# A new order of issue for the attention stage, with longer DMA times, later factor products and a third tile for values

## The chip, the core and the metric

The kernel runs on one core of one Trainium2 chip. The metric is the device time of one execution in microseconds (us), from the chip itself. The core has five engines that each take their instructions in order: TensorE (PE, matrix products and transposes), VectorE (DVE), ScalarE (ACT), GpSimd (POOL) and SyncE (SP), whose only work here is to issue DMAs. An instruction that waits holds back what stands behind it on its engine.

## What is computed

Attention over pooled queries, then a mixture of four experts, then a feed-forward layer with ELU; all in float32:

```python
q_pool = q.reshape(B, H, S // 2, 2, D).mean(axis=3)          # B 2, H 8, S 1152, D 64
scores = np.matmul(q_pool, k.transpose(0, 1, 3, 2)) / np.sqrt(D)
scores = scores - np.max(scores, axis=-1, keepdims=True)
attn = np.exp(scores)
attn = attn / (np.sum(attn, axis=-1, keepdims=True) + 1e-09)
x = np.matmul(attn, v)                                       # then (B*S/2, H*D) = (1152, 512)
for e in range(4):                                           # experts: w1 (512, 1024), w2 (1024, 512)
    out += p[:, e:e + 1] * (np.maximum(x @ w1[e], 0.0) @ w2[e])
h = out @ w_in                                               # (512, 2048)
y = np.where(h > 0.0, h, np.exp(np.minimum(h, 0.0)) - 1.0) @ w_out
```

## The kernel before

The 16 heads are treated as 8 pairs. A pair's 2 x 576 pooled queries are nine blocks of 128; block 4 belongs to both heads. For each block the scores against 1152 keys are made in two parts (z = 0 of 512 columns, z = 1 of 2 x 320), so there are 72 x 2 parts. Every step of the attention has a letter, and each letter a function:

- S `scores` (PE), R `max_all` (DVE, the row maximum of a part), E `exp` (ACT, reads the part from PSUM, 144 of them in all), T `transposes` (PE, three 128 x 128 at a time), D and G `evac` (copies of the transposed blocks to `pt`, on ACT or DVE), V `values` (PE, `pt` with the head's v, in two halves h = 0, 1, line 621), O `output` (ACT or DVE, copies a half of the values from PSUM to the tile `xo`).
- Since the two parts of a row have maxima and sums of their own, each head has a small chain that makes the factors: I (DVE, line 569), U (POOL), J (ACT, exponential of the differences, line 578), K (POOL), M (DVE, reciprocal), N (POOL). The factors must be laid along the free dimension, which is done through DRAM: "3" `factors_out` (SP, `dr<-st`, line 643) and, once that has landed, "4" `factors_in` (SP, two DMAs `fb<-dr`, line 649).
- X `x_scaled` (POOL; DVE for the last two heads) multiplies `xo` by `fb` and adds the two halves, H `x_high` (ACT, `xs<-xo`) rounds the result to the fast format, L `x_low` (POOL) makes the remainder, m `x_out` (SP, four DMAs to `XH` and `XL`) puts both where the experts read them.
- For the next pairs: q and k (SP) load, A, B, C make the high and low part of the queries and r (SP, `Q<-q`, line 488, four DMAs) lays them out; F, W and s (SP, `K<-kh`, `K<-k`, line 505, four DMAs) do so for the keys; v (SP) loads values. w, y, g, f load and split the first weights of the experts.

POOL and DVE copies and products of two tensors come through two helpers, so many of these steps bear line 332 (copy) or 335 (two tensors); the tiles tell them apart.

The order in which all these steps are issued is made by `order_of`, a list scheduler that runs when the kernel is built. `STAGES` gives for each letter the engines that may do it, with the time that the scheduler reckons, and a rank; `LAG` and `LATE` tell how long after its end a step's result is reckoned to be there (SP: the DMA's landing); `MORE` adds to the rank of single steps. The numbers are only the scheduler's: they change no instruction, only its place and, where two engines may do it, its engine. After the attention stand the matrix products of experts and feed-forward (line 798), with `hh` (ACT) and `hl` (DVE) splitting each result; two PSUM tiles take turns there.

Two `xo` tiles took turns by head, so O of a head waited for L of the head two before it.

Of the kernel before, what the change touches and what calls it, by code (L numbers as in the profile page):

```python
# [10 lines left out]
F32 = mybir.dt.float32  # L11
# [7 lines left out]
P = 128  # L19
# [15 lines left out]
    "M": (dict(DVE=200), 1.2),  # L35
    "N": (dict(POOL=400), 1.2),
    "3": (dict(SP=500), 2),
    "4": (dict(SP=950), 2),
    "X": (dict(POOL=2180), 6),
    "T": (dict(PE=327), 2),  # L40
    "D": (dict(ACT=480, DVE=557), -3),
    "G": (dict(ACT=480, DVE=557), -4),
    "V": (dict(PE=2140), 6),
    "O": (dict(ACT=400, DVE=460), 0),
    "H": (dict(ACT=400), 8),
    "L": (dict(POOL=740), 3),
    "a": (dict(POOL=800, DVE=470), 5),
    "b": (dict(ACT=440), 1),
    "c": (dict(DVE=470), 4),
# [3 lines left out]
    "k": (dict(SP=450), -9),  # L53
    "A": (dict(POOL=1430), -4),
    "B": (dict(ACT=690), -4),
    "C": (dict(DVE=1100), -3),
    "r": (dict(SP=1850), -3),
    "F": (dict(ACT=690, DVE=470), -4),
    "W": (dict(POOL=1430), -3),
    "s": (dict(SP=1850), -3),  # L60
    "m": (dict(SP=1850), 8),
    "l": (dict(SP=730), 20),
    "v": (dict(SP=450), -4),
    "w": (dict(SP=730), 20),
    "y": (dict(SP=600), 20),
    "g": (dict(ACT=575), 20),
    "f": (dict(POOL=1365), 20),
# [1 line left out]
}  # L69
WARM = 11  # L70

LAG = {"PE": 190, "ACT": 210, "DVE": 220, "POOL": 210, "SP": 8500}
LATE = {"3": 11000, "4": 8500, "r": 6000, "s": 6000}

MIXED = {"D": dict(ACT=320, DVE=330), "G": dict(ACT=320, DVE=330)}
SECOND = {"S": dict(PE=585), "R": dict(DVE=822), "E": dict(ACT=920), "V": dict(PE=2620)}
# [10 lines left out]
VBANK = "S0", "S0"  # L87

MORE = {
# [16 lines left out]
}  # L106


# [19 lines left out]
def attention_ops(NH, KC):  # L128
# [3 lines left out]
    def op(rank, before, x, *k, after=0):  # L132
        rank += STAGES[x][1] + sum(MORE.get(y, 0) for y in names_of(x, *k))
        ops[(x, *k)] = [b for b in before if b], rank, after
# [27 lines left out]
    for b in range(NB):  # L162
        p, m = divmod(b, MB)

        hs = [2 * p] * (m < 5) + [2 * p + 1] * (m > 3)
        if p:
            need = early = [("r", p), ("s", p)]
        else:
            need = [(x, i, z) for x in "ce" for i in hs for z in range(2)]
            if b < 2:  # L170
                need.remove(("c", 0, 1))
            early = [x for x in need if b > 3 or x != ("e", 0, 1)]
        for z in (0, 1):
            op(b + 0.3 * z, need if z else early, "S", b, z)
            op(b + 0.3 * z, [("S", b, z)], "R", b, z)
            op(b + 0.3 * z, [("R", b, z), *[("T", b - NP, u) for u in U if b >= NP]], "E", b, z)
        for u in U:
            op(b, [("E", b, z) for z in (0, 1) if (z == 0 and 3 * u < CUT) or (z and 3 * u + 3 > CUT)] + [("V", i - 2, 1) for i in hs if i > 1], "T", b, u)
            op(b, [("T", b, u)], "D", b, u)
            if m == 4:  # L180
                op(b, [("T", b, u)], "G", b, u)
        if m in (4, 8):
            i = hs[0]
            for h in (0, 1):
                cs = range(CUT, KC) if h else range(CUT)
                ds = [("D", x, u) for x in blocks_of(i) for u in sorted({c // 3 for c in cs})]
                if i % 2:
                    ds = [("G", *x[1:]) if x[1] == blocks_of(i)[0] else x for x in ds]
                op(b + 0.5 * h, ds + [("V", i, 0) if h else ("v", i)], "V", i, h)
                op(b + 0.5 * h, [("V", i, h)] + [("L", i - 2)] * (i > 1), "O", i, h)  # L190
            op(b, [("E", x, z) for x in range(b - 4 + i % 2, b + 1) for z in (0, 1)], "I", i)
            op(b, [("I", i)], "U", i)
            op(b, [("U", i)], "J", i)
            op(b, [("J", i)], "K", i)
            op(b, [("K", i)], "M", i)
            op(b, [("M", i)], "N", i)
            op(b, [("N", i), i > 1 and ("4", i - 2)], "3", i)
            op(b, [("3", i), i % 2 and ("3", i - 1), i > 1 and ("X", i - 2)], "4", i)
            op(b, [("O", i, 0), ("O", i, 1), ("4", i)], "X", i)
            op(b, [("X", i), i > 1 and ("m", i - 2)], "H", i)  # L200
            op(b, [("H", i)], "L", i)
            op(b, [("L", i)], "m", i)
# [84 lines left out]
def attention_then_moe_then_elu_ffn(  # L287
# [43 lines left out]
    def copy(e, out, a):  # L331
        (nc.scalar.copy if e == "ACT" else engines[e].tensor_copy)(out, a)  # L332

    def tt(e, out, a, b, op):
        engines[e].tensor_tensor(out=out, in0=a, in1=b, op=op)  # L335
# [37 lines left out]
    with ExitStack() as actx:  # L373
# [117 lines left out]
                    )  # L491

        def pair_k_high(e, p, y):
            if y == 0:
                raws["h", p] = raw_p.tile([P, 2, KQ], F32R, tag="k", name="kh")
            copy(e, raws["h", p][:, y], raws["k", p][:, y])

# [130 lines left out]

        xo = [x_p.tile([P, 2, HQ], F32, name="xo%d" % j) for j in range(2)]
        xs = [x_p.tile([P, 2, HQ], F32R, name="xs%d" % j) for j in range(2)]
        fb = [x_p.tile([P, 2 * HQ], F32, name="fb%d" % j) for j in range(2)]

        def output(e, i, h):
            copy(e, xo[i % 2][:, h], tb.pop((i, h))[:, :HQ])

        def factors_out(e, i):
            p, y = divmod(i, 2)
# [12 lines left out]
                )  # L652

        def x_scaled(e, i):
            x = xo[i % 2]
            tt(e, x, x, fb[i % 2].rearrange("p (q z) -> p z q", z=2), ALU.mult)
            tt(e, x[:, 0], x[:, 0], x[:, 1], ALU.add)

        def x_high(e, i):
            copy(e, xs[i % 2][:, 0], xo[i % 2][:, 0])  # L660

        def x_low(e, i):
            x = xs[i % 2]
            tt(e, x[:, 1], xo[i % 2][:, 0], f(x)[:, 0], ALU.subtract)

        def x_out(e, i):
            b, h = heads[i]
# [285 lines left out]
```

## Time and profile before

| | |
|---|---|
| median of 3 runs | 871.22 us (870.48 to 871.96) |
| profiled execution, its own time | 871.93 us |
| its span, first to last instruction | 870.2 us |
| attention, by PE | 0 to 265.2 us |
| experts and feed-forward | 265.2 to 870.2 us |
| PE busy | 850.6 us (98%) |
| DVE, ACT, POOL busy | 473.0, 343.5, 387.8 us |
| mean granted TensorE clock | 0.992 |

A row of the timeline gives the start and length in us, the engine, the line, what is written and read, and in brackets how long the engine had been idle and what ended that. Lines "x3" are several instructions in one row. Everything of the change lies in the attention.

### The profile page before, as it was taken

The numbers are of one execution on the slowest core, as the hardware profiler recorded it, in microseconds if no ns is written. First come the engines' busy times: TensorE is split into PE (matmuls) and PEld (weight loads), VectorE is DVE, ScalarE is ACT, GpSimd is POOL, SyncE is SP. The second block draws the span as 40 slices with busy tenths as digits, with TensorE's granted clock in tenths as the row PEclk, the third lists the DMA queues.
The fourth block names the chain that finished last, engine by engine and source line by source line (L and its number), as shares of the span: only waits on it lengthen the run. The fifth ranks groups of instructions, "written<-read, shape, count | busy, mean of one in ns | idle before, by whom it ended". The sixth has DMA issues, their size and how long they took to land.

```text
span 870.2 us, 13813 instructions
## 1 busy us (share of the span) xinstructions
PE 850.6 (98%) x5374; PEld 793.0 (91%) x5374; DVE 473.0 (54%) x700; ACT 343.5 (39%) x731; POOL 387.8 (45%) x384
## 2 busy tenths in 40 slices
PE   8989999989999999999999999999999999999998
PEld 7767677767768999999999999999999999999998
DVE  8767577666653465564565465465556522333232
ACT  6767686667762312212211221221232243223121
POOL 4343552344323515465554546455454464425321
PEclk9999999999999999999999999999999999999999
DMA  7979858868315424133424315232422311000011
GB/s 255 206 169 198 206 136 190 176 118 206 73 29 168 177 79 160 37 121 122 149 85 132 111 39 173 95 121 98 144 85 86 122 49 49 1 1 1 1 42 69
DMA packets 51457, 97.35 MB, mean 112 GB/s; under 512 B 14912, under 2 KB 29248, under 8 KB 48448
## 3 DMA queue, kind: packets, MB, share of 16 engines
q1 hardware_dynamic: 51392, 96.47, 40.3%
q8 instruction: 42, 0.69, 0.4%
q14 instruction: 23, 0.19, 0.1%
HBM read 64.37 MB, written 10.84 MB: 86 GB/s over the span
## 4 chain that ended last, share of the span: by engine, by line
PE 79%; DMA 9%; POOL 3%; DVE 2%; issue 2%; ACT 2%; SPq 2%; POOLq 0%; DVEq 0%; ACTq 0%
PE p L798 64%; PE t L598 5%; PE s L536 5%; PE s L621 5%; DMA q<-in_q 2%; DMA fb<-dr 2%; DMA Q<-q 2%; POOL xo L335 1%; DMA k<-in_k 1%; POOL acc L853 1%; DMA K<-k 1%; SPq L505 1%; DMA k<-in 1%; ACT e L553 1%; SPq L488 1%
## 5 line engine op out<-in xcount | busy, mean ns | idle before, releaser
L798 PE MATMUL p<-XH,h 128*128 128x384 f32 (+1 forms) x608 | 198.2, 326 | 0.9 <-ACT xo L332 0.5
L798 PE MATMUL p<-XH,l 128*128 128x384 f32 (+1 forms) x608 | 198.0, 326 | 0.0
L798 PE MATMUL p<-XL,h 128*128 128x384 f32 (+1 forms) x608 | 198.0, 326 | 0.0
L798 PE MATMUL p<-hh,l 128*128 128x384 f32 (+1 forms) x608 | 197.9, 326 | 0.0
L798 PE MATMUL p<-hl,h 128*128 128x384 f32 (+1 forms) x608 | 197.9, 326 | 0.0
L798 PE MATMUL p<-hh,h 128*128 128x384 f32 (+1 forms) x608 | 197.9, 326 | 0.0
L335 POOL TENSOR_TENSOR l<-w,h 128x512 fp32r<-128x512 f32 x96 | 125.6, 1326 | 74.2 <-ACT h L332 74.2
L819 ACT ACTIVATE hh<-p 128x768 fp32r<-128x768 f32 (+1 forms) x50 | 39.4, 789 | 280.3 <-PE p L798 280.3
L820 DVE SCALAR_TENSOR_TENSOR hl<-p,hh 128x768 fp32r<-128x768 f32 (+1 forms) x50 | 46.3, 925 | 151.3 <-ACT hh L819 151.3
L798 PEld LDWEIGHTS p<-XH,h 128*128 128x128 f32 x608 | 114.1, 188 | 1.7 <-ACT xo L332 1.0
L798 PEld LDWEIGHTS p<-hh,h 128*128 128x128 f32 x608 | 114.1, 188 | 0.0
L798 PEld LDWEIGHTS p<-hl,h 128*128 128x128 f32 x608 | 114.1, 188 | 0.0
L798 PEld LDWEIGHTS p<-hh,l 128*128 128x128 f32 x608 | 114.1, 188 | 0.0
L798 PEld LDWEIGHTS p<-XL,h 128*128 128x128 f32 x608 | 114.1, 188 | 0.0
L798 PEld LDWEIGHTS p<-XH,l 128*128 128x128 f32 x608 | 114.1, 188 | 0.0
L547 DVE TENSOR_REDUCE st<-s 128x1 f32<-128x512 f32 (+1 forms) x144 | 105.1, 751 | 15.8 <-PE s L536 12.7
L536 PE MATMUL s<-K,Q 128*128 128x320 f32 (+1 forms) x480 | 112.8, 364 | 0.6 <-ACT e L553 0.6
L598 PEld LDWEIGHTS t<-ident,e 128*128 128x128 f32 x648 | 77.4, 144 | 36.4 <-ACT e L553 12.0
L598 PE MATMUL t<-ident,e 128*128 128x128 f32 x648 | 97.3, 282 | 13.3 <-ACT pt L332 7.3
L553 ACT ACTIVATE e<-s,st 128x512 f32<-128x512 f32 (+1 forms) x144 | 107.1, 751 | 1.7 <-DVE st L547 1.6
L772 POOL TENSOR_TENSOR nt<-nt,ne 128x512 f32<-128x512 f32 x32 | 41.8, 1307 | 121.8 <-issue 63.8
L832 POOL TENSOR_TENSOR hl<-e,hh 128x768 fp32r<-128x768 f32 (+1 forms) x26 | 44.8, 1725 | 110.2 <-ACT hh L831 110.1
(68 smaller groups left out, 965.7 us busy)
## 6 DMA issues: line engine op xcount, KB each, us to landing
w<-in_wb SPq DMA_DIRECT2D x8, 1024.0 KB, 6.5
d<-in_va SPq DMA_DIRECT2D x16, 512.0 KB, 4.7
w<-nt SPq DMA_DIRECT2D x32, 256.0 KB, 3.3
d<-in_vb SPq DMA_DIRECT2D x16, 512.0 KB, 4.4
w<-w SPq DMA_DIRECT2D x8, 1024.0 KB, 6.6
Q<-q SPq DMA_DIRECT2D x28, 288.0 KB, 6.2
w<-in_wa SPq DMA_DIRECT2D x7, 1024.0 KB, 6.3
v<-in_v SPq DMA_DIRECT2D x16, 288.0 KB, 6.1
```

The lines of the kernel that those rows point to most:

```text
L335: engines[e].tensor_tensor(out=out, in0=a, in1=b, op=op)
L488: nc.sync.dma_start(out=f(qs[p % 2])[D * r : D * r + D, :, :, half(z)], in_=raws["q", p][D * z : D * z + D],)
L536: nc.tensor.matmul(out=t[:, j], lhsT=q[:, o : o + P], rhs=ks[p % 2][:, y, c : c + PARTS[z][1]], start=k == x == 0, stop=2 * k + x == last,)
L547: nc.vector.tensor_reduce(out=nm[b, z], in_=s_t[b, z], axis=AX.XY, op=ALU.max, negate=True)
L553: nc.scalar.activation(et[b % NP][:, part(z)].rearrange("p (j k) -> p j k", j=PARTS[z][0]), s_t.pop((b, z)), AF.Exp, bias=nm.pop((b, z)), ...
L598: nc.tensor.transpose(t[:, c * P : c * P + P], et[b % NP][:, (3 * u + c) * P : (3 * u + c + 1) * P], ident)
L621: nc.tensor.matmul(out=tb[i, h][64 * z : 64 * z + 64, :HQ], lhsT=raws[i, "v"][:, c, :], rhs=pt[i % 2][:, c, half(z)], start=c == cs[0], st ...
L772: nc.gpsimd.tensor_tensor(out=t, in0=t, in1=e, op=ALU.add)
L798: nc.tensor.matmul(out=ps, lhsT=w[:, c, m * P : m * P + P], rhs=x[:, c], start=c == 0 and w is hi and x is xh, stop=c == 3 and w is lo,)
L819: nc.scalar.activation(oh, s, AF.Relu)
L820: nc.vector.scalar_tensor_tensor(out=ol, in0=s, scalar=0.0, in1=f(oh), op0=ALU.max, op1=ALU.subtract)
L832: nc.gpsimd.tensor_tensor(out=ol, in0=e, in1=f(oh), op=ALU.subtract)
```

## The change

Numbers of the scheduler are changed, and with them the order. The core of the diff:

```diff
-    "4": (dict(SP=950), 2),
-    "X": (dict(POOL=2180), 6),
+    "4": (dict(SP=1700), 2),
+    "X": (dict(POOL=2300), 6),
...
-    "r": (dict(SP=1850), -3),
+    "r": (dict(SP=2400), -3),
...
-LAG = {"PE": 190, "ACT": 210, "DVE": 220, "POOL": 210, "SP": 8500}
-LATE = {"3": 11000, "4": 8500, "r": 6000, "s": 6000}
+LAG = {"PE": 190, "ACT": 210, "DVE": 220, "POOL": 210, "SP": 9500}
+LATE = {"3": 12000, "4": 11500, "r": 8000, "s": 8000, "X": 1200, "U": 900, "K": 700}
...
-                op(b + 0.5 * h, [("V", i, h)] + [("L", i - 2)] * (i > 1), "O", i, h)
+                op(b + 0.5 * h, [("V", i, h)] + [("L", i - 3)] * (i > 2), "O", i, h)
...
-            if y == 0:
+            if ("h", p) not in raws:
...
-        xo = [x_p.tile([P, 2, HQ], F32, name="xo%d" % j) for j in range(2)]
+        xo = [x_p.tile([P, 2, HQ], F32, name="xo%d" % j) for j in range(3)]
...
-            copy(e, xo[i % 2][:, h], tb.pop((i, h))[:, :HQ])
+            copy(e, xo[i % 3][:, h], tb.pop((i, h))[:, :HQ])
```

H, L, C, s, m and w have longer reckoned times too (C a shorter one), the other uses of `xo` count by three, and the table `MORE` is another one throughout. No step is added or left out. All line numbers after 87 grow by one.

Three places show what it makes of the order. On ACT, where head 8 is rounded (`xs<-xo`). Before, that row stands ahead of the exponential of head 10's differences (`st12_119`, step J) and behind 102 of the 144 exponentials of scores (`e..<-s..`):

```order
L553 ACTIVATE e1_98,st11_118<-s10_108,st10_117 128x640
L332 CAST xs0_124<-xo0_122 128x288
L578 ACTIVATE st12_119<-st12_119 128x10
L553 ACTIVATE e0_97,st11_118<-s11_109,st10_117 128x640
L332 COPY pt0_102<-t1_105 128x3x128
L332 COPY pt1_103<-t0_104 128x3x64
L553 ACTIVATE e1_98,st11_118<-s00_106,st10_117 128x512
```

In the changed kernel, at the same head (its `xo` is now the third tile, `xo2`), with two casts of weights (`h<-w`) ahead:

```order
L554 ACTIVATE e3_100,st11_118<-s10_108,st10_117 128x640
L333 CAST h_1759<-w_162 128x512 x2
L333 COPY pt1_103<-t0_104 128x3x128
L579 ACTIVATE st12_119<-st12_119 128x10
L333 CAST xs0_125<-xo2_124 128x288
L333 COPY pt1_103<-t1_105 128x3x128
L554 ACTIVATE e2_99,st01_115<-s00_106,st00_114 128x512
```

The cast has moved behind the exponential of head 10's differences, and stands behind 108 exponentials of scores. Counted in the same way, it moved from 31 to 36 for head 0, from 48 to 57 for head 2 and from 84 to 93 for head 6.

On SP, the first two heads' factors (`dr<-st` out, `fb<-dr` in) among the loads of pairs 2 and 3. Before:

```order
L405 DMA k<-in_k 128x1152
L488 DMA Q_110<-q 64x4x288 x4
L643 DMA dr<-st_116 128x5x2
L405 DMA q<-in_q 128x1152
L409 DMA v<-in_v 128x576
L643 DMA dr<-st_116 128x4x2
L405 DMA q<-in_q 128x1152
L677 DMA p<-in_p 128x36
L505 DMA K_112<-kh 64x2x576 x2
L505 DMA K_112<-k 64x2x576 x2
L649 DMA fb_126<-dr 64x576 x2
L649 DMA fb_127<-dr 64x576 x2
```

In the changed kernel:

```order
L644 DMA dr<-st_116 128x5x2
L410 DMA v<-in_v 128x576
L406 DMA k<-in_k 128x1152
L489 DMA Q_110<-q 64x4x288 x4
L406 DMA q<-in_q 128x1152
L678 DMA p<-in_p 128x36
L644 DMA dr<-st_116 128x4x2
L650 DMA fb_127<-dr 64x576 x2
L406 DMA q<-in_q 128x1152
L506 DMA K_112<-kh 64x2x576 x2
L506 DMA K_112<-k 64x2x576 x2
```

The first head's factors are now read back ahead of the second load of queries and of the copies of keys, no longer behind them; the store of the same factors goes out ahead of pair 2's load of keys.

On DVE, where the attention ends and the experts begin: the products with factors of heads 14 and 15, then the splits `hl` of the experts' first results. Before:

```order
L588 RECIPROCAL st_118<-st_118 128x4
L332 COPY pt_103<-t_104 128x3x128
L335 TENSOR_TENSOR xo_122<-xo_122,fb_126 128x576
L335 TENSOR_TENSOR xo_122<-xo_122 128x288
L335 TENSOR_TENSOR xo_123<-xo_123,fb_127 128x576
L335 TENSOR_TENSOR xo_123<-xo_123 128x288
L820 SCALAR_TENSOR_TENSOR hl<-p_2749,hh 128x2x288
L820 SCALAR_TENSOR_TENSOR hl<-p_2776,hh 128x2x288
```

In the changed kernel:

```order
L589 RECIPROCAL st_118<-st_118 128x4
L336 TENSOR_TENSOR xo_124<-xo_124,fb_127 128x576
L336 TENSOR_TENSOR xo_124<-xo_124 128x288
L821 SCALAR_TENSOR_TENSOR hl<-p_2750,hh 128x2x288
L336 TENSOR_TENSOR xo_122<-xo_122,fb_128 128x576
L336 TENSOR_TENSOR xo_122<-xo_122 128x288
L821 SCALAR_TENSOR_TENSOR hl<-p_2777,hh 128x2x288
```

Head 15's product now stands between the first and the second split. And on SP, in the same place, before:

```order
L643 DMA dr_2553<-st12_119 128x4x2
L649 DMA fb0_126<-dr_2553 64x576 x2
L649 DMA fb1_127<-dr_2553 64x576 x2
L672 DMA XH_67<-xs0_124 64x288
L672 DMA XL_68<-xs0_124 64x288
```

and in the changed kernel:

```order
L644 DMA dr_2598<-st12_119 128x4x2
L650 DMA fb0_127<-dr_2598 64x576 x2
L673 DMA XH_67<-xs1_126 64x288
L673 DMA XL_68<-xs1_126 64x288
L673 DMA XH_67<-xs1_126 64x288
L673 DMA XL_68<-xs1_126 64x288
L650 DMA fb1_128<-dr_2598 64x576 x2
```

Head 15's factors (`fb1`) are read back behind the four DMAs that put out head 13 (`xs1`), whose cast on ACT now stands behind the last copy of values, that of head 15 (`xo`, step O).

## Rows read from the trace of the kernel before

**Rows 1.** The page, first part: busy time, share of the span, instructions by engine

```profile
PE 850.6 (98%) x5374; PEld 793.0 (91%) x5374; DVE 473.0 (54%) x700; ACT 343.5 (39%) x731; POOL 387.8 (45%) x384
```

**Rows 2.** Timeline of PE, 54 to 188 us: all rows with idle time before

```profile
54.79 0.73 PE L536 MATMUL s<-K,Q 128*128 128x512 f32 x2 [0.63 <-ACT e L553]
61.95 0.90 PE L598 MATMUL t<-ident,e 128*128 128x128 f32 x3 [3.16 <-ACT e L553]
...
89.18 0.55 PE L598 MATMUL t<-ident,e 128*128 128x128 f32 x3 [0.49 <-ACT pt L332]
91.00 0.55 PE L598 MATMUL t<-ident,e 128*128 128x128 f32 x3 [1.28 <-ACT pt L332]
...
153.19 1.35 PE L598 MATMUL t<-ident,e 128*128 128x128 f32 x6 [1.97 <-ACT pt L332]
...
187.28 1.31 PE L598 MATMUL t<-ident,e 128*128 128x128 f32 x6 [2.98 <-ACT pt L332]
```

**Rows 3.** Stretches of 40 us: busy by engine, granted clock, DMA share, GB/s

```profile
60.00:100.00 40.00, 36.29 (x241) 28.54 (x243) 25.18 (x48) 28.85 (x76) 19.73 (x32) 0.91 0.83 178
...
140.00:180.00 40.00, 38.03 (x264) 30.65 (x262) 29.19 (x50) 28.98 (x78) 12.99 (x23) 0.96 0.81 164
180.00:220.00 40.00, 37.02 (x255) 28.14 (x254) 24.75 (x50) 28.47 (x76) 20.46 (x36) 0.96 0.70 163
```

**Rows 4.** Timeline of PE: first value product of heads 1, 5, 7, 11

```profile
37.59 2.16 PE L621 MATMUL s<-pt,v 128*64 128x288 f32 x16
...
106.17 2.16 PE L621 MATMUL s<-pt,v 128*64 128x288 f32 x16
...
135.63 2.16 PE L621 MATMUL s<-pt,v 128*64 128x288 f32 x16
...
202.81 2.16 PE L621 MATMUL s<-pt,v 128*64 128x288 f32 x16
```

**Rows 5.** Timeline, 173 to 187 us: head 8's factors, product, cast, next exponential

```profile
173.42 1.11 SPq L649 DMA_DIRECT2D fb<-dr  x2
...
183.11 1.43 POOL L335 TENSOR_TENSOR xo<-xo,fb 128x576 f32<-128x576 f32 x1 [18.22 <-DMA fb<-dr]
...
185.44 0.43 ACT L332 CAST xs<-xo 128x288 fp32r<-128x288 f32 x1 [4.21 <-POOL xo L335]
...
185.99 0.78 ACT L553 ACTIVATE e<-s,st 128x640 f32<-128x640 f32 x1
```

**Rows 6.** Timeline, other engines, at the three earlier stalls

```profile
51.98 1.42 POOL L335 TENSOR_TENSOR q<-q 128x576 f32<-128x576 f32 x1 [5.15 <-DMA p<-in_p]
...
60.68 0.43 ACT L332 CAST xs<-xo 128x288 fp32r<-128x288 f32 x1 [3.79 <-POOL xo L335]
...
87.33 0.43 ACT L332 CAST xs<-xo 128x288 fp32r<-128x288 f32 x1 [1.72 <-POOL xo L335]
...
89.11 0.86 DVE L332 CAST kh<-k 128x576 fp32r<-128x576 f32 x2 [3.58 <-DMA k<-in_k]
...
151.35 0.43 ACT L332 CAST xs<-xo 128x288 fp32r<-128x288 f32 x1 [3.21 <-POOL xo L335]
```

**Rows 7.** Timeline, 263 to 272 us: from the attention to the experts

```profile
263.19 1.09 SPq L649 DMA_DIRECT2D fb<-dr  x2
...
264.75 0.40 ACT L332 COPY xo<-s 128x288 f32<-128x288 f32 x1 [1.97 <-PE s L621]
...
265.20 0.40 PE L798 MATMUL p<-XH,h 128*128 128x288 f32 x1 [0.50 <-ACT xo L332]
...
267.64 0.76 DVE L335 TENSOR_TENSOR xo<-xo,fb 128x576 f32<-128x576 f32 x1
...
270.27 0.59 SPq L672 DMA_DIRECT2D XL<-xs  x1
...
270.44 0.76 DVE L820 SCALAR_TENSOR_TENSOR hl<-p,hh 128x576 fp32r<-128x576 f32 x1 [1.05 <-ACT hh L819]
...
271.83 0.65 ACT L819 ACTIVATE hh<-p 128x576 fp32r<-128x576 f32 x1 [1.42 <-PE p L798]
```

More of the change, by code (lines that the diff above doesn't have):

```diff
@@ L44 @@
     "O": (dict(ACT=400, DVE=460), 0),
-    "H": (dict(ACT=400), 8),
-    "L": (dict(POOL=740), 3),
+    "H": (dict(ACT=440), 8),
+    "L": (dict(POOL=810), 3),
     "a": (dict(POOL=800, DVE=470), 5),
@@ L55 @@
     "B": (dict(ACT=690), -4),
-    "C": (dict(DVE=1100), -3),
-    "r": (dict(SP=1850), -3),
+    "C": (dict(DVE=800), -3),
+    "r": (dict(SP=2400), -3),
     "F": (dict(ACT=690, DVE=470), -4),
     "W": (dict(POOL=1430), -3),
-    "s": (dict(SP=1850), -3),
-    "m": (dict(SP=1850), 8),
+    "s": (dict(SP=2800), -3),
+    "m": (dict(SP=2300), 8),
     "l": (dict(SP=730), 20),
     "v": (dict(SP=450), -4),
-    "w": (dict(SP=730), 20),
+    "w": (dict(SP=1700), 20),
     "y": (dict(SP=600), 20),
@@ L654, in x_scaled @@
         def x_scaled(e, i):
-            x = xo[i % 2]
+            x = xo[i % 3]
             tt(e, x, x, fb[i % 2].rearrange("p (q z) -> p z q", z=2), ALU.mult)
@@ L659, in x_high @@
         def x_high(e, i):
-            copy(e, xs[i % 2][:, 0], xo[i % 2][:, 0])
+            copy(e, xs[i % 2][:, 0], xo[i % 3][:, 0])
         def x_low(e, i):
             x = xs[i % 2]
-            tt(e, x[:, 1], xo[i % 2][:, 0], f(x)[:, 0], ALU.subtract)
+            tt(e, x[:, 1], xo[i % 3][:, 0], f(x)[:, 0], ALU.subtract)
         def x_out(e, i):
```

33 rows, old and new, of the table MORE are left out of this document.

## The prediction

> **What bounds the kernel now.** I read the page's busy times first, then the rows in which PE had been idle, then the granted clock by stretches, and last the other engines around each gap. PE is busy for 98% of the span [rows 1], so only two things can be won: its idle time, and time in which it ran at the lower clock. Between 54 and 188 us six rows show all its idle time there: 0.63 + 3.16 + 0.49 + 1.28 + 1.97 + 2.98 = 10.5 us, each ended by an exponential or a copy on ACT [rows 2]. The clock falls in the same places: 0.91, 0.96 and 0.96 in the three stretches of 40 us that hold the four stalls [rows 3], and it is whole in the others. A clock of 1.2 instead of 2.4 GHz for 9%, 4% and 4% of 40 us is 40 x 0.17 = 6.8 us. So the stalls cost about 17.3 us. A second view agrees: the same value product of heads 5 and 7, a pair apart with no stall between, stands 29.46 us apart; from head 1 to head 11, five pairs, it takes 165.22 us [rows 4], which is 165.22 - 5 x 29.46 = 17.9 us more than five undisturbed pairs. I count 17.3 and leave the odd 0.6.
>
> What stands behind the gaps is the same thing four times. At 187 us: head 8's factors are asked for at 173.42, POOL waits for them until 183.11, ACT has meanwhile reached the cast of the product and stands 4.21 us, and the exponential that PE needs stands right behind that cast [rows 5]. At 60.68, 87.33 and 151.35 the cast of heads 0, 2 and 6 waits 3.79, 1.72 and 3.21 us for POOL; at 89 us DVE also waits 3.58 us for pair 4's keys [rows 6]. Waits of 4.21 and 3.21 on ACT became 2.98 and 1.97 on PE [rows 2, 5, 6]: about 1.24 us of each is covered by what PE has in hand.
>
> **The change part by part.** *The cast later.* No instruction is added. Eighteen exponentials go by in 29.46 us, so one is 1.64 us [rows 4]. By the order, the cast of heads 0, 2, 6 and 8 moves back by 5, 9, 9 and 6 exponentials: 8.2, 14.7, 14.7 and 9.8 us. Against it goes the later issue of the factors' DMA on SP, which I count by the score parts that precede, on PE, the last thing that SP must wait for there: 20 becomes 22, 37 becomes 39, 73 becomes 76, 92 becomes 94, so 3.3, 3.3, 4.9 and 3.3 us. With the wait to be covered that leaves 8.2 - 3.3 - 3.79 = 1.1 us, 14.7 - 3.3 - 1.72 = 9.7, 14.7 - 4.9 - 3.21 = 6.6 and 9.8 - 3.3 - 4.21 = 2.3 us to spare. Head 0's is more than that, since its DMA no longer stands behind a load that waits for a free tile and behind the eight copies of queries and keys; all four waits go. What is behind the cast on ACT is then no longer held; behind the cast itself wait x_low on POOL and four DMAs on SP, and nothing that PE needs within a pair.
>
> *Keys of pair 4.* Their cast on DVE moves behind 58 row maxima instead of 50, 13.1 us; the load moves behind a load of values that waits for a value product ending at about 87 us, where it was issued at about 80: 7 us. 13.1 - 7 - 3.58 leaves 2.5 us. This wait goes too.
>
> *The clock.* It fell in the stretches with the four large gaps of PE and in no others [rows 2, 3]. With the gaps gone I take the 6.8 us as gained.
>
> *The third tile and the later products.* Output of a head waits for x_low three heads back instead of two. With casts later by 5 to 9 exponentials that is what keeps the tile from becoming the new wait; by itself I cost it at nothing, since in all pairs without a late DMA PE shows no idle row. Products on POOL stand further behind in its queue, ahead of the sums and reciprocals of the next heads at a few places (head 2 and 3's two products in a row, 4.5 us). The reciprocals on DVE that wait for POOL there stand beside value products of 2.16 us and more [rows 4], which cover them. If that cover were gone, each would cost PE its length less 1.24 us.
>
> *First 24 us.* The order there changes too. DVE sets the pace, and up to the thirteenth row maximum the same DVE work stands in it but for one cast given to ACT, some 0.4 us. I count nothing, with 1.5 us either way.
>
> *The end of the attention.* Here the change adds a wait. Head 15's factors are asked for behind the four DMAs of head 13, whose cast now stands behind the last output copy on ACT. That copy ends at 265.15 [rows 7]. In the time of the kernel before: cast 0.43 and four issues of about 0.6 us with x_low between, so the factors are asked for at about 268.4, where it was 263.19. From that to the product it was 267.64 - 263.19 = 4.45 us, so the product starts at 272.85, takes 1.2 to 1.75 us, and the second `hl`, which now stands behind it on DVE and lasts 0.76, ends at about 275.4. PE needs that PSUM tile for its fourth group: two groups end before 271.83 [rows 7], some 3.2 us each, so at 274.7. That gives 0.7 to 0.8 us of new idle time. Its bounds: none, if the factors come 0.8 us sooner; and 6.0 us, if they take the 9.7 us that they took at 173.42 [rows 5]. I take 0.8, because the 4.45 us are from the same place, where few other DMAs run. The first `hl` stays ahead of the product, and the experts' own loads, behind head 15's DMAs on SP, come about 4 us later, at the second of their uses.
> The Trainium skill's page "DMA: Bandwidth & Descriptors" (section "Anatomy of one DMA") gives one DMA, there fitted for GpSimd's, a fixed 2.0 us and its bytes at 436 GB/s. By it an estimate for these 147 KB is 2.3 us; the end would then cost nothing and the time would be 0.8 us less. Both rows here differ from it.
>
> **Sum.** The profiled execution took 871.93 us, of which 870.2 are its span; that is 0.7 above the median of 871.22. 871.93 - 10.5 - 6.8 + 0.8 = 855.4, and from the median 871.22 - 16.5 = 854.7 us.
>
> **The rivals.**
> 1. *The loads of the first pairs.* Pair 4's queries are now asked for behind head 0's factors, and POOL adds them between the differences and the sum of head 2. In the kernel before, POOL stood 5.15 us for them, until 51.98 [rows 6] (the row names a small load issued right behind them). If they land some 2 us later than that, the reciprocal of head 2 on DVE waits, and the first stall stays: 0.63 + 3.16 us and half of the first stretch's clock loss, 1.8, so 5.6 us: 860.3. For it: the DMA share there is the highest. Against: nothing but two factor DMAs was put ahead of it.
> 2. *The spare is too small.* Heads 0 and 8 have 1.1 and 2.3 us. If factors land later than they did by more than that plus the cover of 1.24, each stalls again, by about 1 us and a fall of the clock of 1.7 (6.8 / 4): 5.4 us together, 860.1.
> 3. *The end.* Factors of head 15 that take 9.7 us: 5.2 us more and one fall of the clock, 861.7.
> 4. *POOL becomes the bound of each pair's end, and it is slower.* POOL's run there (two splits of keys, a product, the sums of two heads) holds a reciprocal on DVE, and row maxima stand behind it. At a stall like that at 187 us, 2.98 + 1.7 = 4.7 us at each of seven pair ends is 32.8 us, so 887.5. It decides from 2.6 us for each, idle and clock together, because 7 x 2.6 = 18.2 is the gain and the 0.2%; so from a wait of about 2.1 us on DVE. Against it: POOL is busy 45% [rows 1], and in the pair from 106 to 136 us its waits left no idle row on PE.
>
> **How the numbers follow.** The forecast has 0.66, with a range of its own from 851.5 (no new wait at the end, 1.5 us from the start, the odd 0.6) to 858. Rival 1 has 0.12, rival 2 0.10, rival 3 0.08, rival 4 0.04. The range from 851.5 to 862.5 takes in the forecast and the first three. A measurement of this kernel can tell about 0.2% from no change, 1.7 us. All cases but the fourth are faster by more than that: 0.96. Rival 4 gives 0.03 to slower and 0.01 to no change.
>
> **What would show it.** PE's rows with idle time between 40 and 250 us should be gone or under 0.6 us, the granted clock should be 1.00 in every stretch, and the value products of all pairs should stand 29.5 us apart. Casts of products on ACT should have no idle time ahead that ends with POOL, and POOL's products none that ends with a factor DMA. The matrix products of the experts should begin some 17 us earlier, with one gap of about 0.8 us some 9.5 us later, ended by `hl`. Wrong would be: a fall of the clock anywhere after 40 us, reciprocals on DVE that wait over 2 us for POOL with PE idle behind them, or a long wait of DVE for the last factors.

## The result, and the profile after

The changed kernel takes 856.45 us (median of 4 runs, 855.12 to 857.05), the kernel before 870.85 us beside it: a ratio of 0.9842 (95% interval 0.9819 to 0.9865), 14.4 us less. The forecast was 854.7 us, 16.5 less. Of the profiled executions one took 871.93 us and the other 857.05, 14.9 us apart; the account below is of these two.

The page's first lines, against [rows 1] (busy time, share of the span, instructions by engine):

```profile
span 855.2 us, 13804 instructions
...
PE 844.9 (99%) x5374; PEld 788.7 (92%) x5374; DVE 474.4 (55%) x713; ACT 340.5 (40%) x718; POOL 390.0 (46%) x384
```

The timeline of PE, with the rows that had idle time between 40 and 200 us, against the 10.5 us of [rows 2], and the row at which the experts begin:

```profile
83.31 0.73 PE L537 MATMUL s<-K,Q 128*128 128x512 f32 x2 [1.17 <-ACT xo L333]
93.16 0.86 PE L537 MATMUL s<-K,Q 128*128 128x320 f32 x4 [0.24 <-ACT e L554]
152.41 0.85 PE L537 MATMUL s<-K,Q 128*128 128x320 f32 x4 [0.24 <-ACT e L554]
...
250.29 0.40 PE L799 MATMUL p<-XH,h 128*128 128x288 f32 x1 [0.50 <-ACT xo L333]
```

The stretches of [rows 3] again (length, busy by engine, granted clock, DMA share, GB/s):

```profile
60.00:100.00 40.00, 38.59 (x279) 28.81 (x275) 27.81 (x52) 29.07 (x77) 19.75 (x33) 1.00 0.92 184
140.00:180.00 40.00, 39.76 (x289) 30.65 (x286) 29.12 (x55) 32.16 (x83) 19.09 (x30) 1.00 0.80 200
180.00:220.00 40.00, 39.76 (x292) 30.33 (x291) 28.27 (x55) 29.14 (x78) 18.51 (x39) 1.00 0.62 127
```

The four stalls are gone, and the clock is whole. The experts begin at 250.29 instead of 265.20, 14.9 us earlier, and from there on both kernels take the same 605 us: the whole gain lies in the attention. One stall is new, at 83 us; its rows on the other engines are

```profile
80.84 1.41 POOL L336 TENSOR_TENSOR q<-q 128x576 f32<-128x576 f32 x1 [10.25 <-DMA q<-in_q]
...
82.28 0.68 ACT L443 ACTIVATE q<-q 128x576 fp32r<-128x576 f32 x1 [2.81 <-POOL q L336]
...
83.00 0.76 DVE L481 SCALAR_TENSOR_TENSOR q<-q 128x576 fp32r<-128x576 f32 x1 [3.82 <-ACT q L443]
```

These are pair 5's queries: POOL sums them as soon as they land, ACT and DVE have reached the two steps behind that sum and stand.

To see where time is lost when no row is idle, I also laid out each kernel's attention as 229.8 us of undisturbed PE work (0.47 and 0.585 us for the two parts of a block, 0.327 for three transposes, 2.09 and 2.58 for the two halves of values, from undisturbed rows) and read how far the trace was behind that line. Five of the experiments below stand beside the two kernels: the kernel before with three tiles and four casts late, the same with three products late too, the changed kernel with these products put back, with two tiles, and with the old table. All columns creep by some 0.02 to 0.05 us per us, since the durations are a little short. Each column is one execution, the profiled one; that with late casts took 868.09 us, the fastest of its ten.

| us behind, at PE work of | before | after | casts late | products and casts late | products back | two tiles | old table |
|---|---|---|---|---|---|---|---|
| 24 | 11.3 | 11.0 | 11.3 | 10.7 | 10.8 | 11.0 | 13.5 |
| 64 | 17.7 | 11.7 | 13.3 | 13.2 | 11.6 | 11.9 | 15.6 |
| 88 | 22.0 | 14.4 | 23.0 | 23.8 | 20.3 | 14.8 | 16.8 |
| 128 | 22.8 | 15.3 | 23.8 | 24.6 | 21.2 | 17.3 | 19.4 |
| 152 | 27.1 | 16.2 | 25.8 | 25.3 | 23.5 | 19.3 | 20.0 |
| 176 | 32.5 | 16.9 | 28.6 | 26.0 | 24.1 | 21.7 | 20.9 |
| 224 | 34.9 | 19.4 | 31.0 | 28.4 | 27.2 | 26.7 | 24.4 |

### The profile page after: what moved, and what is told of

It is laid out like the page before. It is cut to its first block, busy times and chain, and to the rows that moved or that the text cites. A ratio compares the mean times of both kernels' runs of the same rounds, so it can differ in the third digit from the quotient of the medians.

```text
span 855.2 us, 13804 instructions
## 1 busy us (share of the span) xinstructions
PE 844.9 (99%) x5374; PEld 788.7 (92%) x5374; DVE 474.4 (55%) x713; ACT 340.5 (40%) x718; POOL 390.0 (46%) x384
## 4 chain that ended last, share of the span: by engine, by line
PE 85%; DMA 6%; ACT 3%; DVE 2%; issue 2%; POOL 1%; SPq 1%; DVEq 0%; ACTq 0%; POOLq 0%
PE p L799 65%; PE s L622 7%; PE s L537 7%; PE t L599 6%; DMA q<-in_q 2%; DMA Q<-q 1%; DMA K<-k 1%; ACT e L554 1%; POOL acc L854 1%; ACT pt L333 1%; DMA q<-in 1%; DVE nt L758 0%; SPq L489 0%; ACT XH L781 0%; DVE e L829 0%
## 5 line engine op out<-in xcount | busy, mean ns | idle before, releaser
L548 DVE TENSOR_REDUCE st<-s 128x1 f32<-128x512 f32 (+1 forms) x144 | 105.4, 751 | 17.7 <-PE s L537 14.6
L537 PE MATMUL s<-K,Q 128*128 128x320 f32 (+1 forms) x480 | 110.0, 357 | 1.9 <-ACT xo L333 1.2
L599 PEld LDWEIGHTS t<-ident,e 128*128 128x128 f32 x648 | 75.4, 140 | 23.7 <-issue 6.1
L599 PE MATMUL t<-ident,e 128*128 128x128 f32 x648 | 94.3, 276 | 2.7 <-ACT e L554 2.0
```

The costliest lines, as they stand in the source:

```text
L537: nc.tensor.matmul(out=t[:, j], lhsT=q[:, o : o + P], rhs=ks[p % 2][:, y, c : c + PARTS[z][1]], start=k == x == 0, stop=2 * k + x == last,)
L548: nc.vector.tensor_reduce(out=nm[b, z], in_=s_t[b, z], axis=AX.XY, op=ALU.max, negate=True)
L599: nc.tensor.transpose(t[:, c * P : c * P + P], et[b % NP][:, (3 * u + c) * P : (3 * u + c + 1) * P], ident)
```

## The experiments

All kernels are edits of one of the two. Where single steps were moved, the scheduler's finished list was edited: a step stands ahead of the exponential with the number given (there are 144), or ahead of the step named. Ratios are to the kernel before on the same chip, with 95% intervals; its medians there were 870.1 to 871.3 us.

### Tile and casts, from the kernel before

The prediction said that the cast on ACT, moved later, ends the stalls, and that the third tile alone is worth nothing.

```diff
-        xo = [x_p.tile([P, 2, HQ], F32, name="xo%d" % j) for j in range(2)]
+        xo = [x_p.tile([P, 2, HQ], F32, name="xo%d" % j) for j in range(3)]
```

> The kernel before, with three xo tiles instead of two, its order of issue unchanged. Theory (the stalls are the cast on ACT that stands ahead of its product, and the third tile only makes room for a later cast): no change, 871 us within 1.5, the same four gaps of PE. Rival (the output copy that waits for a free tile is itself part of the stalls): some of the gaps shrink, 2 us or more faster.

Measured: 870.71 us, 1.0005 (0.9985 to 1.0025). As expected.

```diff
+    ("H", 2): 52, ("L", 2): 53, ("m", 2): 54,
+    ("H", 6): 88, ("L", 6): 89, ("m", 6): 90,
+    ("H", 8): 106, ("L", 8): 107, ("m", 8): 108,
```

> The kernel before with two xo tiles, and only the casts of heads 2, 6 and 8 (with their remainder and output DMAs) 4 exponentials later, which is as late as two tiles allow; head 0's can't move by more than one and stays. Four exponentials are 6.5 us, against waits of 1.72, 3.21 and 4.21 us. Theory: the stalls of heads 6 and 8 go, 3.6 + 4.6 = 8.2 us; head 0's stays, and pair 4's late keys on DVE keep the gap of 1.28 us at 91: 862 to 863.5 us. If the cast alone made the gaps at 89 and 91, 859 us. Rival (it is the earlier DMAs of the changed order, or the third tile, that end the stalls): 871 us within 2.

Measured: 876.86 us, 1.0077 (1.0047 to 1.0107): slower, where neither the theory nor its rival had that.

```diff
+    ("H", 0): 36, ("L", 0): 37, ("m", 0): 38,
+    ("H", 2): 57, ("L", 2): 58, ("m", 2): 59,
+    ("H", 6): 93, ("L", 6): 94, ("m", 6): 95,
+    ("H", 8): 108, ("L", 8): 109, ("m", 8): 110,
```

> The kernel before with three xo tiles and the casts of heads 0, 2, 6 and 8 moved back to where the changed kernel has them (behind 36, 57, 93 and 108 exponentials), nothing else moved: all DMAs are issued where they were. Theory: the stalls of heads 0, 6 and 8 go, 5.6 + 3.6 + 4.6 = 13.8 us, and that of pair 4's keys on DVE stays: 857 to 858.5 us. If the keys make no gap of their own: 853.5 us. Rival (earlier factor DMAs are needed too): head 0's stall stays in part, 860 us or more.

Measured: 870.86 us, 1.0008 (0.9987 to 1.003): nothing won.

```diff
+    ("F", 4, 0): 52, ("F", 4, 1): 52,
+    ("W", 4, 0): 53, ("W", 4, 1): 53, ("s", 4): 55,
```

> As the one with three tiles and four later casts, and pair 4's keys split 4 exponentials later as well (their copies to K with them); five steps of 1276 and what hangs on them are moved, the DMA times and the table stay those of the kernel before. Theory: all four stalls go, 17.3 to 17.9 us: 853 to 854.5 us, a little faster than the changed kernel. Rival (what the stalls cost comes back elsewhere, since the engines have no more room): 856 us or more, with new gaps of PE.

Measured: 870.34 us, 1.0004 (0.998 to 1.0029). So the theory of the prediction fell as a whole: three edits that were to win 7 to 18 us won nothing. It held at one place, head 0: with three tiles and four late casts its two rows (0.63 and 3.16 us) are gone, though its product still stood 2.93 us for the factors. At heads 6 and 8 that run kept 0.96 and 1.77 of the 1.97 and 2.98 us, and around 90 us 1.77 us became 6.77. The timelines say why. With three late casts and two tiles (head 8; POOL, ACT, PE):

```profile
184.96 1.41 POOL L359 TENSOR_TENSOR xo<-xo,fb 128x576 f32<-128x576 f32 x1 [21.29 <-DMA fb<-dr]
...
187.20 0.47 POOL L359 TENSOR_TENSOR st<-st,st 128x5 f32<-128x5 f32 x2
...
187.70 0.21 ACT L602 ACTIVATE st<-st 128x10 f32<-128x10 f32 x1 [7.70 <-POOL st L359]
...
189.11 1.54 PE L622 MATMUL t<-ident,e 128*128 128x128 f32 x6 [6.03 <-ACT pt L356]
```

The product that waits for the factors holds POOL's queue, and behind it stand the differences of head 10 (`st`), for which ACT's exponential (step J) waits, with the exponentials of scores behind that. The same with three tiles and four late casts (head 2 on POOL and ACT, PE, pair 4's keys on DVE; then head 8 on ACT and PE):

```profile
84.75 1.41 POOL L362 TENSOR_TENSOR xo<-xo,fb 128x576 f32<-128x576 f32 x1 [15.48 <-DMA fb<-dr]
...
87.50 0.21 ACT L605 ACTIVATE st<-st 128x10 f32<-128x10 f32 x1 [6.26 <-POOL st L362]
...
88.91 0.90 PE L625 MATMUL t<-ident,e 128*128 128x128 f32 x3 [4.60 <-ACT pt L359]
...
90.11 0.83 DVE L359 CAST kh<-k 128x576 fp32r<-128x576 f32 x2 [8.96 <-DMA k<-in_k]
...
183.31 0.21 ACT L605 ACTIVATE st<-st 128x10 f32<-128x10 f32 x1 [3.44 <-POOL st L362]
...
184.71 0.88 PE L625 MATMUL t<-ident,e 128*128 128x128 f32 x6 [1.77 <-ACT pt L359]
```

At head 0 no such step is held: by the order, head 2's differences stand ahead of head 0's product on POOL. And these edits are not of the casts alone. They moved the casts' output DMAs too, so not all DMAs were issued where they were, as an expectation has it: head 2's factors were asked for at 77.55 us (before 76.60), although the work ahead of them ran some 4 us sooner (table).

### Products on POOL

The second theory: the place that counts is that of the product on POOL, ahead of or behind the next head's sums. Three tests of it: products and casts late in the kernel before, with three tiles and with two (only the moves of products are shown), and in the changed kernel three products moved forward to their old places while the casts stay late.

```diff
+    ("X", 0): ("N", 2), ("X", 2): 53, ("X", 6): ("X", 7), ("X", 8): ("X", 9),
```

> As the kernel of before with three tiles and four later casts, and now the products on POOL of heads 2, 6 and 8 later too, behind the sums of the head that follows them (behind 53, 88 and 106 exponentials, as in the changed kernel). Second theory: a product that waits for its factors holds POOL, and behind it on POOL stand the differences and sums of the next head, for which ACT and DVE wait; so the stalls of heads 0, 6 and 8 and the first of the two gaps at 89 go, and only pair 4's late keys on DVE stay (a gap of 1.3 to 3 us and 1.8 us of clock): 857 to 860 us. First theory (the cast on ACT): 871 us as without it. Rival (POOL's order makes no difference, the factors themselves come too late): 866 us or more.

Measured: 866.53 us, 0.9946 (0.9921 to 0.9971), 4.3 us less than with the casts alone, but not the 857 to 860 expected. PE has no gap above 0.3 us left at heads 0, 6 and 8.

```diff
+    ("X", 2): 51, ("X", 6): 87, ("X", 8): 105,
```

> The kernel before with two tiles, casts of heads 2, 6 and 8 four exponentials later as in the run that took 876.9 us, and now their products on POOL behind the next head's sums (behind 51, 87 and 105 exponentials). Second theory: the stalls of heads 6 and 8 go, head 0's (5.6 us) and the keys' stay: 861 to 865 us, 12 us or more less than with the casts alone. First theory: 876 us. Rival (with two tiles a later product holds the output copy, which waits for the remainder, and PSUM with it): 868 us or more, with DVE or ACT waiting for POOL ahead of a copy to xo.

Measured: 867.15 us, 0.9956 (0.993 to 0.9982): 9.7 us less than with the casts alone, where 12 or more were expected.

```diff
+    ("X", 2): 46, ("X", 6): 82, ("X", 8): 100,
```

> The changed kernel with nothing undone but the place on POOL of three products: those of heads 2, 6 and 8 stand again where they were, behind 46, 82 and 100 exponentials, the first two ahead of the next head's differences and sums. The casts stay late. Second theory: head 4's sums wait for head 2's factors, which land at 87.6 us, 5.4 us after those differences ran, and head 8's for head 6's (143.4, 3.2 us after), each 2.2 us more for the product: two stalls of 3 to 5 us with a fall of the clock of 1.7 each, 864 to 869 us. First theory: the casts have over 5 us to spare, so 856.5 us within 1.5.

Measured: 865.65 us, 0.9932 (0.9908 to 0.9956), 9.2 us slower than the changed kernel. One stall came back, longer than in the kernel before (POOL, ACT, PE), the second with 0.93 us of idle PE. The test is harder than the kernel before: the factors' read-back stays at its new place, so these products stand 1, 3 and 4 exponentials behind it, where they stood 7. So it shows that the product's place counts, and 9.2 us is not what that place cost before.

```profile
87.45 1.41 POOL L354 TENSOR_TENSOR xo<-xo,fb 128x576 f32<-128x576 f32 x1 [6.22 <-DMA fb<-dr]
...
90.20 0.21 ACT L597 ACTIVATE st<-st 128x10 f32<-128x10 f32 x1 [6.68 <-POOL st L354]
...
90.67 1.54 PE L617 MATMUL t<-ident,e 128*128 128x128 f32 x6 [4.17 <-ACT pt L351]
```

The complement is the changed kernel with late products and its casts earlier again, close behind their products (not at their old places, which lie ahead of these):

```diff
+    ("H", 0): 34, ("H", 2): 55, ("H", 3): 57, ("H", 4): 74, ("H", 5): 78,
+    ("H", 6): 90, ("H", 7): 96, ("H", 9): 114, ("H", 11): 131,
```

> The changed kernel, in which nine casts (heads 0, 2 to 7, 9 and 11) stand 1 to 4 exponentials earlier on ACT again, two exponentials behind their product, as the kernel before mostly had them; the products, and all else, stay in their late places. In the changed kernel the casts had 1.6 to 6.5 us between the end of their product and their own start, and lose 1.6 to 6.6 us of it here. If the product's place on POOL is what carries the gain, as the run with three products back showed: 856.5 us within 1.5, with ACT waiting less than 1 us ahead of any cast. First theory (the cast's place): stalls come back, 860 us or more.

Measured: 857.38 us, 0.9832 (0.9816 to 0.9848), no difference from the changed kernel's 0.9842. Only head 0's cast waited over 1 us (1.67), and PE has a gap of 1.25 us there, at 60.64. The stall at 83 us is absent. The view of the tile `fb` sums it up: how long POOL's products had stood for factors between 20 and 250 us, in all and how many times, in the kernel before, in the changed one, and in it with three products put back:

```profile
  POOL xo L335: 51.9, 6
```
```profile
  POOL xo L336: 0.7, 1
```
```profile
  POOL xo L354: 17.2, 4
```

### Why products and casts gave only 4.5 us

With products and casts late in the kernel before, PE has no stall left between 60 and 250 us but one above 0.5 us, which is larger than any before it (DVE, POOL, PE; then the stretch with its clock). The first row names a load of values, issued at 86.24; the keys' own load was issued at 79.81 and landed just as the row begins:

```profile
90.31 0.83 DVE L363 CAST kh<-k 128x576 fp32r<-128x576 f32 x2 [9.25 <-DMA v<-in_v]
...
88.30 1.40 POOL L366 TENSOR_TENSOR q<-q 128x576 f32<-128x576 f32 x1 [7.53 <-DMA q<-in_q]
...
92.17 0.90 PE L629 MATMUL t<-ident,e 128*128 128x128 f32 x3 [7.62 <-ACT pt L363]
```

```profile
80.00:100.00 20.00, 12.38 (x77) 9.37 (x76) 7.09 (x16) 8.27 (x23) 9.81 (x14) 0.74 0.63 122
```

The table shows it as well: at 64 us of work that kernel is 4.5 us ahead of the kernel before, at 88 us 1.8 us behind it. Pair 4's keys and pair 5's queries came no sooner, though all that precedes them ran sooner. SP shows why: the output DMAs of head 0, moved along with its cast, now stand ahead of them (the load of keys is issued at 79.81, before at 80.06):

```profile
73.06 0.54 SPq L703 DMA_DIRECT2D XH<-xs  x1
74.13 0.46 SPq L703 DMA_DIRECT2D XL<-xs  x1
75.47 0.46 SPq L703 DMA_DIRECT2D XH<-xs  x1
76.85 0.46 SPq L703 DMA_DIRECT2D XL<-xs  x1
77.36 1.24 SPq L680 DMA_DIRECT2D fb<-dr  x2
78.70 0.52 SPq L674 DMA_DIRECT2D dr<-st  x1
79.27 0.50 SPq L436 DMA_DIRECT2D q<-in_q  x1
79.81 0.43 SPq L436 DMA_DIRECT2D k<-in_k  x1
```

A third theory: any step that stands on its engine before its DMA has landed stalls; so move all that were seen to wait.

```diff
+    ("A", 5): ("X", 2), ("B", 5): 56, ("C", 5): 57,
+    ("F", 4, 0): 54, ("F", 4, 1): 54, ("W", 4, 0): 55, ("W", 4, 1): 55, ("s", 4): 56,
+    ("F", 5, 0): 71, ("F", 5, 1): 71, ("W", 5, 0): 72, ("W", 5, 1): 72, ("s", 5): ("k", 6),
+    ("F", 6, 0): 87, ("F", 6, 1): 87, ("W", 6, 0): ("X", 6), ("W", 6, 1): ("X", 6), ("s", 6): 89,
+    ("F", 7, 0): 104, ("F", 7, 1): 104, ("W", 7, 0): 105, ("W", 7, 1): 105,
```

> The kernel before with three tiles, its numbers and its table, and an edit of its order in which every step that was seen to wait for a DMA stands later on its engine: the products and casts of heads 0, 2, 6 and 8 as in the run that took 866.5 us, and now also the splits of pair 4's keys (behind 54 exponentials instead of 48) and those of pairs 5 to 7 that follow from it, and the sum and scalings of pair 5's queries (the sum behind head 4's factors). Third theory (what stalls is any step whose place on its engine comes before its DMA has landed, one as much as the other, and removing some lets the next one show): the gap of 7.6 us and its 5.2 us of clock go too, 853.5 to 857 us, level with the changed kernel. Rival (the DMAs themselves must be issued earlier, which only the remade order does): 860 us or more, with a gap at the next load.

Measured: 872.91 us, 1.0024 (1.0 to 1.0049). The rival's time came. The gap at 90 is gone, and others stand behind it, the longest at 120 and 166 us (ACT and PE):

```profile
118.86 0.43 ACT L385 CAST xs<-xo 128x288 fp32r<-128x288 f32 x1 [6.40 <-DMA XH<-xs]
...
120.60 1.54 PE L651 MATMUL t<-ident,e 128*128 128x128 f32 x6 [5.06 <-ACT pt L385]
...
166.05 0.90 PE L651 MATMUL t<-ident,e 128*128 128x128 f32 x3 [2.50 <-ACT pt L385]
```

The copies of pair 4's keys go out later (from 103.69 us, from 99.36 in the run without these moves), so on SP the next load of keys is issued only at 112.46, head 2's output behind it from 112.90, and head 4's cast waits for that output's tile. A step moved by hand moves its DMAs in SP's queue, and so the next pair's. The rival's reason is not borne out: the changed kernel does not issue these DMAs earlier on the whole. Pair 5's queries go out at 71.18 us instead of 79.69, but head 2's factors at 81.54 instead of 76.60 and pair 4's keys at 86.66 instead of 80.06. Head 2's product and the split of pair 4's keys moved back further than that: they stand 8 and 9 exponentials behind the issue of what they wait for, instead of 7 and 7. Why the remade order holds through all pairs where this one does not is thus shown only in part.

### What the remade order needs

The changed kernel without its third tile, the order made anew:

```diff
-                op(b + 0.5 * h, [("V", i, h)] + [("L", i - 3)] * (i > 2), "O", i, h)
+                op(b + 0.5 * h, [("V", i, h)] + [("L", i - 2)] * (i > 1), "O", i, h)
```

> The changed kernel with all its numbers and its table, but two xo tiles, and so an order made under the rule that an output copy waits for the remainder two heads back. The order then has products nearly as late (5 to 10 exponentials behind the factors' read-back, changed kernel 7 to 10), casts up to 6 exponentials earlier and pair 4's keys 5 exponentials behind their load instead of 9. If the third tile only makes room: some stalls come back, most likely pair 4's keys, 858 to 864 us. If the third tile is worth nothing by itself: 856.5 within 1.5. If the order hangs on it: 866 us or more.

Measured: 864.8 us, 0.9942 (0.992 to 0.9965), just over the 858 to 864 expected for a tile that makes room; but no stall came back. Its longest idle row of PE after 40 us and before the experts is 0.75 us, its clock is 1.00 throughout, and it falls behind little by little from 88 us of work on (table). The table of ranks stayed that of the three-tile kernel; what two tiles would take with one of their own was not tried, so the 8.4 us are not the tile's alone.

```diff
-    "v": 6.5, "c01.0": -3.5, "c01.0a": -4, "v.1": -9, "a10.0": 11.5, "c10": 7.5, "c10.0": 4,
...
+    "v": 6.5, "c01.0a": -6.5, "c10": -2, "c10.0": -8, "d10.0": -5.5, "d10.0a": -4, "B": -10.5,
```

> The changed kernel (three tiles, longer reckoned times) with the table of single ranks of the kernel before. Its products stand 6 to 11 exponentials behind the factors' read-back, where the kernel before had 5 to 7. Third theory: the reckoned DMA times carry most of the gain, 856 to 862 us. Rival (the table, fitted place by place, carries it): 866 us or more.

Measured: 864.27 us, 0.9936 (0.991 to 0.9961). With the longer reckoned times and the old table all four stalls are gone and the clock is 1.00, as the third theory has it, but 2.3 us more than expected remain: 2.5 us are lost in the first 24 us of work, more in small pieces later (table), and at the start of the experts a gap of 1.57 us ended by `hl`.

### The new stall at 83 us

```diff
+    ("A", 5): ("X", 2), ("B", 5): 54, ("C", 5): 54,
```

> The changed kernel with pair 5's query sum on POOL behind head 4's sums, and its two scalings on ACT and DVE 6 exponentials later, nothing else. Theory: the stall at 83 us (POOL waited 10.25 us for these queries, ACT 2.81 and DVE 3.82 behind it) goes, 1.2 us of idle PE and up to 2.5 us with the slow rows around it: 854 to 855.3 us, which would be faster than both kernels. Rival (head 2's product, now behind that sum, is the next that is late): 856 us or more.

Measured: 857.26 us, 0.9837 (0.98 to 0.9874). The rival's time: the gap at 83 is gone, PE shows 0.24 and 0.73 us at 92 and 94 instead, and the span is the same 855.2 us. In this kernel the DMA share between 40 and 100 us is 0.99, 1.01 and 0.99 by stretches of 20. By the table's reckoning it is 13.9 us behind at 88 us of work, the changed kernel 14.4, and the run with the casts earlier again, which stood at 60.64 and not at 83, 14.2. Something common may set the pace up to there, the loads for one; that was not tested. No version was found that beats the changed kernel.

## Why the prediction was right, and where its reasons were not

**What bounds the kernel, and the price of the stalls:** right. The four stalls with their low clock were the gain: 10.5 and 6.8 us were forecast, and between 40 and 176 us of work the kernel before fell 20.9 us behind, the changed one 5.7. One reading is off without harm to the sum: with two levels of the clock, a mean of 0.91 is the lower one for 18% of the stretch, not 9%; the time lost is the 9%.

**The mechanism ("The cast later"):** this step failed at three of the four stalls. It named one chain: late factors, late product, waiting cast, exponentials behind the cast. In the trace of before a second one runs beside it at heads 2, 6 and 8 and is as long. Head 8's product ran at 183.11 [rows 5]; behind it on POOL, and then on ACT between the cast at 185.44 and the exponential at 185.99, in a row that [rows 5] does not show:

```profile
185.37 0.48 POOL L335 TENSOR_TENSOR st<-st,st 128x5 f32<-128x5 f32 x2
...
185.88 0.21 ACT L578 ACTIVATE st<-st 128x10 f32<-128x10 f32 x1
```

POOL's differences for head 10 and the cast end within 0.05 us of each other (185.85 and 185.87), and the second row, ACT's step J, needs those differences. A cast taken out of the first chain leaves the second (870.86 us in all), but for head 0; products moved forward cost 9.2 us while the casts have room; casts moved up to their late products cost nothing that can be told (857.38). Late products with the casts at their old places were not run: a cast reads what its product writes, so it would have to wait for it. The prediction had seen that products stand further behind on POOL, and costed that at nothing; it looked there only for what the move might harm. The price was read off the gaps and not off the chain, and the change did both moves: that the sum came out right all the same is luck.

**The spares.** The forecast counted 1.1, 9.7, 6.6 and 2.3 us between factors and cast for heads 0, 2, 6 and 8. In the trace of after, the cast starts 3.0, 5.5, 6.1 and 5.2 us behind its product's end. Rival 2, the spare too small, did not come. The 3.3 us for head 2's later read-back were too few: by the table's reckoning it is asked for at 69.5 us of PE's work, before at 58.7, so 10.8 us later.

**Keys of pair 4.** The forecast set their wait at 3.58 us and left 2.5 to spare, as a side matter. They do not wait in the changed kernel; but with products and casts alone cured they hold PE for 7.62 us, so this part is no side matter.

**The third tile and the table.** The tile alone is worth nothing, as forecast (870.71), and up to 8.4 us in the remade order (864.8); the text had said without a price that it makes room there. The reckoned times with the old table end the stalls; the table itself, which the prediction did not price, is worth 7.8 us, most of it in small pieces.

**Loads of the first pairs (rival 1).** Right in kind, one pair off: it named pair 4's queries, and pair 5's were late. By the table the changed kernel loses 2.7 us between 64 and 88 us of work, of which 1.17 are idle time. That, some 2.2 beyond the creep, is about the 2.4 us by which the attention's gain (14.9) fell short of 17.3, though taking the stall away won nothing (857.26), so the queries are not shown to be the cause; it was not asked where each pair's query steps had gone, though ACT's had moved forward by 5 exponentials (53 to 48).

**The end.** The 0.8 us did not come. Everything stands as worked out, but the term was mis-sized: the factors' DMA was issued 3.0 us after the experts' first product (forecast 3.2), the product followed 3.7 us later, not 4.45, and took 1.2 us, the lower of the two durations. In the rows of DVE, the second `hl` ends at 258.96, 8.7 us after the experts began; PE needs it after some 9.8, by the two runs that follow. It is a near thing: in two of the edits that leave this place as it is, PE has the gap, 0.57 us (products back) and 0.43 us (casts back), ended by `hl` some 10.3 us after the experts began.

```profile
253.33 1.18 SPq L650 DMA_DIRECT2D fb<-dr  x2
...
257.04 0.76 DVE L336 TENSOR_TENSOR xo<-xo,fb 128x576 f32<-128x576 f32 x1 [1.79 <-DMA fb<-dr]
...
258.21 0.75 DVE L821 SCALAR_TENSOR_TENSOR hl<-p,hh 128x576 fp32r<-128x576 f32 x1
```

The estimate of 2.3 us by the Trainium skill (page "DMA: Bandwidth & Descriptors", section "Anatomy of one DMA") would have given the right cost here, none, though the trace does not agree with its duration: these two took 2.9 and 3.1 us from issue to landing, and all factors' DMAs of this kernel 2.9 to 8.3.

**POOL as the bound (rival 4).** It did not come, and its argument, a next step held by POOL's queue, was near the mechanism of the kernel before rather than a risk of the changed one. It named the reciprocal on DVE, but at head 8 that was held until 187.95, when PE had already resumed at 187.28 [rows 2]; what ACT needed was step J.

## What to carry to other kernels

When an engine waits for a late transfer, list everything behind the waiting instruction on its own queue and on the queues that wait for those, before naming one victim; two chains of equal length hide behind each other, and curing one leaves the other, as at heads 2, 6 and 8 here. A step moved by hand takes its DMAs along in the issuing queue, and the next loads with them: a stall cured in one pair came back in the next as long as the order was not made anew with honest transfer times. And a move costed "at nothing" is worth one more question: what did its old place cost?

## What the runs showed of the hardware

What a stall costs in clock was taken as 1.7 us each. It was larger with longer gaps: beside the 2.98 us of before the clock was 0.91 over 20 us (1.8 us), beside 4.17 us in the run with products put back 0.83 (3.4 us), beside 6.03 us in that with three late casts 0.83 as well, beside 7.62 us 0.74 (5.2 us). In stretches of 5 us around that last gap, in which PE did nothing from 85 to 90:

```profile
85.00:90.00 5.00, 0.00 (x0) 0.00 (x0) 0.00 (x0) 0.00 (x0) 1.62 (x3) 0.66 0.93 291
90.00:95.00 5.00, 2.83 (x9) 2.33 (x10) 3.68 (x10) 2.16 (x6) 4.12 (x7) 0.50 0.14 25
95.00:100.00 5.00, 5.00 (x34) 4.14 (x34) 2.50 (x4) 3.61 (x10) 3.68 (x4) 0.81 0.53 113
```

The clock was at its lower level, 1.2 GHz, for all of the 5 us in which PE took its work up again. Of two gaps of nearly one length, 1.97 us in the kernel before and 1.96 us in the one with casts and keys moved, the first went with 0.91 over 20 us and the second with 1.00, so a single gap of that length does not tell whether the clock falls.

The kernel before scattered more than the changed one: 866.6 to 875.6 us in 81 runs beside the experiments, against 855.1 to 858.0 for the changed kernel and the one with casts put back (9 runs together, so part of this is their number). The kernel before also has the waits on DMAs, 51.9 us of them ahead of POOL's products against 0.7; that these cause the scatter was not tested, and the runs with two tiles and with the old table, which have none of the four stalls, span 4.6 and 4.1 us in 10 and 9 runs.
